# First batch's q and k read as four tokens to a partition and turned by products with the identity

## The chip, the cores and the metric

One core of a Trainium2 chip runs the whole program. The metric is the device time of one execution in microseconds; the time of a kernel is the median of its runs. Times inside an execution come from the hardware profiler, counted from the first instruction.

## The reference

Three stages follow one another on 2304 tokens (4 batches of 576), all in float32:

```python
scores = (q @ k^T) / sqrt(64)                    # q, k, v: 4 batches, 8 heads, 576 tokens, 64 wide
cum    = cumsum(log(clip(f, 1e-4, 1)))           # along the tokens of a head
attn   = softmax(causal(scores + cum[i] - cum[j])) 
x      = (attn @ v) with heads side by side      # 2304 x 512
h      = x @ moe_w_in;  y = (h * tanh(softplus(h))) @ moe_w_out
out    = max(y @ w1, y @ w2, y @ w3) @ moe2_w_out
```

The inputs moe_w_in and the other weights come as 64-bit floats and are converted on the chip.

## The kernel before

The attention runs over 16 jobs, each a pair of heads of one batch; jobs 0 to 3 are the first batch. Here they are called pair 0, pair 1 and so on; pair 4 is the first of the second batch. The steps of a pair:

- `load` (L253) issues the pair's loads on SyncE's queue. For k and then q, two transfers of 128 KB, one for each head (L258), bring the first 512 tokens into the tile raw: 128 partitions hold token p of each of four groups of 128 tokens, so each descriptor moves one token of one head, 64 floats or 256 bytes. The two heads lie side by side in every group. A transfer of 32 KB (L262) brings the last 64 tokens. Then come the decay rows, broadcast to all partitions from cum_d, a scratch tensor that the opening computes from f: c2 (L272, two transfers of 256 KB) and c4 (L275, two of 144 KB), both named cb in the profile. raw and both cb tiles have two buffers, so pair 2 is loaded into what pair 0 has released, and so on.
- `prep` (L301) turns k and q on TensorE: four 128 x 128 transposes into one PSUM bank (L312, tile tr), each of which turns both heads of a group of tokens, and one transpose of the last 64 tokens (L313). ScalarE copies the bank to SBUF (L314, tiles kT and qT: head 0 in partitions 0 to 63, head 1 in 64 to 127, tokens in order along the free dimension). Then v is loaded (L319, L323), and GpSimd masks the decay rows (L295, L299).
- `scores` (L338) multiplies q and k in pieces (L336, tile sc); VectorE adds the decay and finds the row's extreme (L390, it reads cb), ScalarE takes the exponent (L396), VectorE the reciprocals of the sums (L357, L358), GpSimd scales the rows (L360, tile P).
- `av` (L404) transposes P on TensorE (L429, tile pp), copies it to SBUF (L433, L435) and multiplies with v (L415, tile av). The two heads' products write partitions 0 to 63 and 64 to 127 of one bank. A float32 product stands in the trace as two MATMULs, a transpose as one.

Beside the attention `load_w_in` (L198) fetches moe_w_in (L146, tile wr), and converts it: ScalarE takes the high words (L156, which reads every second word), GpSimd and VectorE do the rest (L160 to L170). Two such steps are traced per step of the attention, until all is loaded; the fetches are placed behind the latest split of an attention result on VectorE (`pace`).

Once the 512 tokens of the first block have their attention, products with moe_w_in (L181 to L183) fill TensorE beside the further attention; then follow the two other stages. Before that the opening has no other work for TensorE than the attention of the first batch.

The order of instructions on each engine and queue is not written out by hand: the framework's scheduler orders them by priority along a simulated timeline, when the kernel is built. Each engine and SyncE's queue then work through their list in order, each waiting where it must.

The edit lies in `load` and `prep`; the lines that the steps of the prediction touch are L258 to L275, L312, L314, L156, L146, L336, L390 and L415.

```python
raws = [[ap_.tile([128, 640], F32, name=f"raw{c}{i}") for c in "qk"] for i in range(2)]
c2 = as_.tile([128, 2, 7, 128], F32, name="cb", bufs=2)
c4 = as_.tile([128, S], F32, name="cb4", bufs=2)
```

Of the kernel before, what the change touches and what calls it, by code (L numbers as in the profile page):

```python
# [13 lines left out]
AF = mybir.ActivationFunctionType  # L14
# [50 lines left out]
def tile_decay_attention__mish_ff__max3_ff(  # L65
# [16 lines left out]
    nc = tc.nc  # L82
# [19 lines left out]
    ident = const.tile([128, 128], F32, name="ident")  # L102
# [73 lines left out]
    def queued(last):  # L176
        return tc.issue_after(last[-1].ins) if last else ExitStack()
# [52 lines left out]
    def att_psum(name):  # L230
        return aps.tile([128, 512], F32, name=name, tag="ps", bufs=3)

    U, L = slice(0, 64), slice(64, 128)
# [19 lines left out]
    def load(i, b, hp):  # L253

        raw = raws[i % 2]
        for dst, src in ((raw[1], k), (raw[0], q)):
            for h in range(2):
                nc.sync.dma_start(  # L258
                    dst[:, 0:512].rearrange("p (t h d) -> p t h d", h=2, d=64)[:, :, h],
                    src[b, 2 * hp + h, 0:512, :].rearrange("(t p) d -> p t d", t=4),  # L260
                )
            nc.sync.dma_start(  # L262
                dst[U, 512:640].rearrange("p (h d) -> p h d", h=2),
                src[b, 2 * hp:2 * hp + 2, 512:S, :].rearrange("h p d -> p h d"),
            )
        r = b * H + 2 * hp


        c2 = as_.tile([128, 2, 7, 128], F32, name="cb", bufs=2)
        for t in range(2):  # L270
            src = cum_d[r:r + 2, t * 256:t * 256 + 256][None].to_broadcast([128, 2, 256])
            nc.sync.dma_start(c2[:, :, 3 * t:3 * t + 2, :].rearrange("p h t c -> p h (t c)"), src)  # L272
        c4 = as_.tile([128, S], F32, name="cb4", bufs=2)
        for h, rows in enumerate((U, L)):
            nc.sync.dma_start(c4[rows], cum_d[r + h:r + h + 1, :].to_broadcast([64, S]))  # L275
        return dict(i=i, b=b, hp=hp, cb=(c2, c4), raw=raw)
# [15 lines left out]
    def mask_decay(J):  # L292
        c2, c4 = J["cb"]
        for n, src, dst in ((2, 0, 5), (1, 3, 2), (1, 4, 4)):
            nc.gpsimd.affine_select(  # L295
                out=c2[:, :, dst:dst + n, :], in_=c2[:, :, src:src + n, :], pattern=[[0, 2], [0, n], [-1, 128]],
                compare_op=ALU.is_ge, fill=-1e30, base=0, channel_multiplier=1,
            )
        nc.gpsimd.tensor_tensor(out=c4[:, 512:S], in0=c4[:, 512:S], in1=mask4, op=ALU.add)  # L299

    def prep(J):  # L301

        b, hp, raw = J["b"], J["hp"], J["raw"]
        qq = as_.tile([128, 512], F32, name="qT", bufs=2)
        kk = as_.tile([128, S], F32, name="kT", bufs=2)
        last, v_ = q4[J["i"] % 2], vs[J["i"] % 3]
        rest = att_psum("tr")
        for i, dst in ((1, kk), (0, qq)):
            tr = att_psum("tr")
            with queued(last_av):  # L310
                for c in range(4):
                    nc.tensor.transpose(tr[:, c * 128:c * 128 + 128], raw[i][:, c * 128:c * 128 + 128], ident)  # L312
                last_tr[:] = [nc.tensor.transpose(rest[:, i * 64:i * 64 + 64], raw[i][U, 512:640], ident[U, U])]  # L313
            nc.scalar.activation(dst[:, 0:512], tr, AF.Copy)  # L314
        nc.scalar.activation(kk[:, 512:S], rest[:, 64:128], AF.Copy)
        for h, rows in enumerate((U, L)):
            nc.scalar.activation(last[rows, h * 64:h * 64 + 64], rest[rows, 0:64], AF.Copy)
        for h in range(2):
            nc.sync.dma_start(  # L319
                v_[:, h * 256:(h + 1) * 256].rearrange("p (t d) -> p t d", t=4),  # L320
                v[b, 2 * hp + h, 0:512, :].rearrange("(t p) d -> p t d", t=4),
            )
        nc.sync.dma_start(  # L323
            v_[L, 512:640].rearrange("p (h d) -> p h d", h=2),
            v[b, 2 * hp:2 * hp + 2, 512:S, :].rearrange("h p d -> p h d"),
        )
        J.update(q=qq, q4=last, k=kk, vs=v_)
        mask_decay(J)
# [123 lines left out]
    def attention():  # L452


        jobs = [(b, hp) for b in range(B) for hp in range(H // 2)]
        J = {0: load(0, *jobs[0])}
        yield 0
        prep(J[0])
        J[1] = load(1, *jobs[1])
        tok = 0  # L460
        units = [(ji, g) for ji in range(len(jobs)) for g in range(2)]
        pend = []
        for n in range(len(units) + LEAD):
            if n == 6 + LEAD:
                eps.clear()
                early.close()
                eps_h.append(sa.enter_context(tc.tile_pool(name="hps", bufs=2, space=PSUM, reuse_waits="tile")))
            if n < len(units):
                ji, g = units[n]
                pend.append((J[ji], g, scores(J[ji], g)))  # L470
            if n >= LEAD:
                unit = pend.pop(0)
                rest = av(*unit)
                next(rest)
                if unit[0]["b"] == 0:
                    next(rest, None)
            last_tr.clear()
            if n < len(units) and g == (ji == 0) and ji + 1 < len(jobs):
                prep(J[ji + 1])
            if n >= LEAD:  # L480
                next(rest, None)
                if unit[0]["hp"] == H // 2 - 1:
                    tok = unit[0]["b"] * S + (256, S)[unit[1]]
            if n < len(units):
                if g == 1 and ji + 2 < len(jobs):
                    J[ji + 2] = load(ji + 2, *jobs[ji + 2])
            yield tok
# [340 lines left out]
    for t0 in (BLK2, BLK2 + 2 * HALF):  # L828
        hh = [hp2.tile([128, 2 * HALF], F32R, name=f"hh{c}") for c in range(NF2)]
        hl = [hp2.tile([128, 2 * HALF], F32R, name=f"hl{c}") for c in range(NF2)]  # L830
        for p in range(3):
            fs = slice(p * 128, p * 128 + 128)
            for m in range(3):
                S = []
                for k in range(4):
                    t = sst.tile([128, 2, 2, 128], F32R, name="s")
# [49 lines left out]
            for i, eng in ((0, "pool"), (2, "dve"), (1, "dve"), (3, "dve")) if p == 2 else ((i, "pool") for i in range(4)):  # L886
                f, h = p + 3 * (i // 2), i % 2
# [37 lines left out]
```

## Time and profile before

| what | value |
|---|---|
| median of 3 runs | 909.84 us (909.51 to 910.46) |
| the profiled execution's own time | 909.78 us |
| its span, first to last instruction | 907.7 us |
| mean granted TensorE clock | 0.992 |
| busy: TensorE, VectorE, ScalarE, GpSimd | 97%, 55%, 44%, 26% |

How to read the rows further down. PE is TensorE, PEld its weight load, DVE VectorE, ACT ScalarE, POOL GpSimd, SP SyncE; SPq is SyncE's queue of DMA issues. In a row of a timeline stand the start in us, the time in us (from the first to the end of the last of the instructions merged in it), engine, line, operation, out<-in, the size, and the count; in brackets the idle time before it and what ended it. In the stretches each engine's busy us and number of instructions are followed by PEclk, the clock that TensorE was granted (1.00 is 2.4 GHz, 0.50 is 1.2 GHz), by the mean busy share of the 16 DMA engines, and by GB/s. In the rows by line three numbers of ns are the shortest, the median and the longest.

### The profile page before, as it was taken

The numbers are of one execution on the slowest core, as the hardware profiler recorded it, in microseconds if no ns is written. First come the engines' busy times: TensorE is split into PE (matmuls) and PEld (weight loads), VectorE is DVE, ScalarE is ACT, GpSimd is POOL, SyncE is SP. The second block draws the span as 40 slices with busy tenths as digits, with TensorE's granted clock in tenths as the row PEclk, the third lists the DMA queues.
The fourth block names the chain that finished last, engine by engine and source line by source line (L and its number), as shares of the span: only waits on it lengthen the run. The fifth ranks groups of instructions, "written<-read, shape, count | busy, mean of one in ns | idle before, by whom it ended". The sixth has DMA issues, their size and how long they took to land.

```text
span 907.7 us, 13930 instructions
## 1 busy us (share of the span) xinstructions
PE 882.8 (97%) x4800; PEld 704.8 (78%) x4800; DVE 497.1 (55%) x1186; ACT 400.7 (44%) x913; POOL 232.7 (26%) x317
## 2 busy tenths in 40 slices
PE   6898999999999999999999999999999999999998
PEld 3565666767767778889888888889888998889986
DVE  3598675344444343991367575775855447424440
ACT  4687666454443432533465545553433222412211
POOL 3689987222222220000020000000121332013310
PEclk8989999999999999999999999999999999999999
DMA  7896664444333115863456666663499444333401
GB/s 183 227 226 171 179 192 117 115 134 127 105 102 108 47 48 178 292 226 128 143 181 217 214 216 222 217 226 98 162 359 322 124 123 117 111 96 126 139 23 60
DMA packets 125030, 145.25 MB, mean 160 GB/s; under 512 B 64736, under 2 KB 78048, under 8 KB 124960
## 3 DMA queue, kind: packets, MB, share of 16 engines
q1 hardware_dynamic: 105856, 102.41, 39.0%
q10 hardware_dynamic: 16416, 27.79, 8.3%
q0 software_dynamic: 2688, 14.16, 4.3%
q8 instruction: 38, 0.62, 0.3%
q14 instruction: 32, 0.26, 0.1%
HBM read 102.83 MB, written 41.49 MB: 159 GB/s over the span
## 4 chain that ended last, share of the span: by engine, by line
PE 89%; POOL 3%; DMA 2%; DVE 2%; issue 1%; ACT 1%; SPq 1%; POOLq 0%
PE y L181 7%; PE y L183 7%; PE y L182 7%; PE h L181 7%; PE h L182 7%; PE h L183 7%; PE q L182 6%; PE q L183 6%; PE q L181 6%; PE sc L336 5%; PE av L415 5%; PE pp L429 5%; PE o L181 3%; PE o L182 3%; PE o L183 3%; PE g L181 2%
## 5 line engine op out<-in xcount | busy, mean ns | idle before, releaser
L181 PE MATMUL h<-xh,wi 128*128 128x512 f32 (+1 forms) x320 | 121.4, 380 | 1.6 <-ACT he L522 1.3
L182 PE MATMUL h<-xl,wi 128*128 128x512 f32 (+1 forms) x320 | 120.6, 377 | 1.8 <-DVE xl L137 1.8
L183 PE MATMUL h<-xh,wi 128*128 128x512 f32 (+1 forms) x320 | 120.7, 377 | 0.0
L182 PE MATMUL y<-gl,wo 128*128 128x512 f32 (+1 forms) x320 | 117.7, 368 | 0.0
L183 PE MATMUL y<-gh,wo 128*128 128x512 f32 (+1 forms) x320 | 117.6, 368 | 0.0
L181 PE MATMUL y<-gh,wo 128*128 128x512 f32 (+1 forms) x320 | 106.3, 368 | 0.0
L360 POOL TENSOR_SCALAR P<-P,rr 128x128 f32<-128x128 f32 (+3 forms) x128 | 74.0, 592 | 87.5 <-DVE rr L358 31.5
L659 DVE TENSOR_TENSOR gl<-g,gh 128x512 fp32r<-128x512 f32 x72 | 50.0, 697 | 83.3 <-ACT gh L658 83.1
L396 ACT ACTIVATE P<-P,mn 128x128 f32<-128x128 f32 (+3 forms) x128 | 70.7, 554 | 53.4 <-DVE mn L390 50.2
L652 ACT ACTIVATE g<-g 128x512 f32<-128x512 f32 x72 | 45.2, 632 | 70.6 <-DMA g<-h_d 65.7
L181 PEld LDWEIGHTS h<-xh,wi 128*128 128x128 f32 x320 | 60.1, 188 | 14.6 <-issue 2.2
L182 PEld LDWEIGHTS h<-xl,wi 128*128 128x128 f32 x320 | 60.1, 188 | 14.0 <-issue 2.8
L183 PEld LDWEIGHTS h<-xh,wi 128*128 128x128 f32 x320 | 60.3, 188 | 11.5 <-issue 2.7
L182 PEld LDWEIGHTS y<-gl,wo 128*128 128x128 f32 x320 | 60.3, 188 | 10.2
L183 PEld LDWEIGHTS y<-gh,wo 128*128 128x128 f32 x320 | 60.2, 188 | 10.1
L181 PEld LDWEIGHTS y<-gh,wo 128*128 128x128 f32 x320 | 60.3, 189 | 10.1
L522 ACT ACTIVATE he<-h 128x512 f32<-128x512 f32 x56 | 33.3, 595 | 57.0 <-PE h L183 52.4
L851 DVE TENSOR_TENSOR u<-q,p 128x448 f32<-128x448 f32 x36 | 22.4, 621 | 62.3 <-PE q L183 60.7
L336 PE MATMUL sc<-kT,qT 64*128 64x128 f32 (+3 forms) x256 | 51.9, 500 | 3.6 <-DVE mn L390 3.3
L429 PE MATMUL pp<-ident,P 128*128 128x128 f32 x320 | 51.1, 285 | 4.0 <-ACT qT L314 3.6
L658 ACT ACTIVATE gh<-g 128x512 fp32r<-128x512 f32 x72 | 45.0, 627 | 22.0 <-PE y L183 20.9
L429 PEld LDWEIGHTS pp<-ident,P 128*128 128x128 f32 x320 | 37.0, 143 | 20.1 <-issue 5.0
(141 smaller groups left out, 1850.3 us busy)
## 6 DMA issues: line engine op xcount, KB each, us to landing
g<-h_d SPq DMA_DIRECT2D x72, 256.0 KB, 2.9
s<-s_d SPq DMA_DIRECT2D x72, 256.0 KB, 3.0
h_d<-he ACTq DMA_DIRECT2D x56, 256.0 KB, 2.9
wr<-in_moe_w_out_dram SPq DMA_DIRECT2D x22, 512.0 KB, 4.6
wr<-in_moe_w_dram SPq DMA_DIRECT2D x24, 384.0 KB, 3.8
s_d<-sk POOLq DMA_DIRECT2D x12, 768.0 KB, 5.8
cb<-cum_d SPq DMA_DIRECT2D x32, 256.0 KB, 4.2
wr<-in_moe_w_in_dram SPq DMA_DIRECT2D x16, 512.0 KB, 4.5
```

The costliest lines, as they stand in the source:

```text
L181: nc.tensor.matmul(ps, wh, xh, start=start, stop=False, skip_group_check=True)
L182: nc.tensor.matmul(ps, wh, xl, start=False, stop=False, skip_group_check=True)
L183: return nc.tensor.matmul(ps, wl, xh, start=False, stop=stop, skip_group_check=True)
L336: nc.tensor.matmul(dst, lhs, J["k"][rows, c0:c0 + w], start=True, stop=True, skip_group_check=True)
L360: nc.gpsimd.tensor_scalar(made[ci], made[ci], rr[:, ci:ci + 1], 1.0, op0=ALU.mult, op1=ALU.mult)
L396: nc.scalar.activation(Pt, Pt, AF.Exp, scale=-1.0, bias=mn[:, col - 1:col], accum_out=sm[:, ci:ci + 1],)
L415: last = nc.tensor.matmul(acc[(U, L)[h], off:off + w], J["vs"][:, n * 64:n * 64 + 64], T[:, at[h]:at[h] + w], start=kt == 0 and off == 0, ...
L429: turn = nc.tensor.transpose(pp[:, n * 128:n * 128 + 128], Pt[:, k0:k0 + 128], ident)
L522: nc.scalar.activation(he, h, AF.Copy)
L652: nc.scalar.activation(g, g, AF.Mish)
L658: on_act[:] = [nc.scalar.activation(gh, g, AF.Copy)]
L659: on_dve[:] = [nc.vector.tensor_tensor(out=gl, in0=g, in1=gh, op=ALU.subtract)]
```

## The change

For jobs of the first batch (b is 0) the transfers of q and k's first 512 tokens place four consecutive tokens in one partition, 256 floats or 1 KB in a row, head by head in the two halves of the tile. The transpose of 128 columns then no longer holds both heads of one group; instead each of the four tokens of each head is turned by a float32 product with the identity (64 columns of weights, 128 moving columns), which writes the half of the bank that belongs to the head. In the bank the columns then stand as token-in-four first; the copy out of PSUM reads them in order and writes them with a step of four words, so that kT and qT hold what they held before. The last 64 tokens, the later batches and all else stay.

```diff
         for dst, src in ((raw[1], k), (raw[0], q)):
             for h in range(2):
+                if b == 0:
+                    nc.sync.dma_start(
+                        dst[:, h * 256:h * 256 + 256],
+                        src[b, 2 * hp + h, 0:512, :].rearrange("(p t) d -> p (t d)", t=4),
+                    )
+                    continue
                 nc.sync.dma_start(
                     dst[:, 0:512].rearrange("p (t h d) -> p t h d", h=2, d=64)[:, :, h],
                     src[b, 2 * hp + h, 0:512, :].rearrange("(t p) d -> p t d", t=4),
...
                 for c in range(4):
-                    nc.tensor.transpose(tr[:, c * 128:c * 128 + 128], raw[i][:, c * 128:c * 128 + 128], ident)
+                    cs = slice(c * 128, c * 128 + 128)
+                    if b:
+                        nc.tensor.transpose(tr[:, cs], raw[i][:, cs], ident)
+                        continue
+                    for h, rows in enumerate((U, L)):
+                        part = raw[i][:, h * 256 + c * 64:h * 256 + c * 64 + 64]
+                        nc.tensor.matmul(tr[rows, cs], part, ident, start=True, stop=True, skip_group_check=True)
...
-            nc.scalar.activation(dst[:, 0:512], tr, AF.Copy)
+            if b:
+                nc.scalar.activation(dst[:, 0:512], tr, AF.Copy)
+            else:
+                nc.scalar.activation(
+                    dst[:, 0:512].rearrange("r (p c) -> r c p", c=4), tr.rearrange("r (c p) -> r c p", c=4), AF.Copy
+                )
```

## Rows read from the trace of the kernel before

**Rows 1.** Busy us of TensorE, its share of the span, instructions.
```profile
PE 882.8 (97%) x4800; PEld 704.8 (78%) x4800; DVE 497.1 (55%) x1186; ACT 400.7 (44%) x913; POOL 232.7 (26%) x317
```

**Rows 2.** Stretches of the opening: busy us by engine, clock, DMA.
```profile
10.00:20.00 10.00, 6.75 (x24) 3.77 (x22) 3.28 (x19) 4.78 (x17) 3.17 (x7) 0.72 0.98 233
41.77:45.38 3.61, 0.00 (x1) 0.00 (x1) 1.04 (x5) 2.45 (x7) 2.33 (x3) 0.97 1.03 367
45.20:51.50 6.30, 6.12 (x27) 4.37 (x27) 6.12 (x21) 5.65 (x19) 4.14 (x4) 0.50 1.05 238
```

**Rows 3.** The chain of waits from 37 to 44 us: start, us, what.
```profile
37.07 0.59 SPq L146
...
37.70 6.46 DMA wr<-in_moe_w_in_dram
```

**Rows 4.** Timelines of ScalarE and TensorE around 42 to 46 us.
```profile
42.48 0.66 ACT L156 ACTIVATE wt<-wr 128x512 f32<-128x512 f32 x1 [3.85 <-DMA wr<-in_moe_w_in_dram]
...
45.38 1.11 PE L429 MATMUL pp<-ident,P 128*128 128x128 f32 x4 [3.61 <-ACT qT L314]
```

**Rows 5.** Timeline of SyncE's queue, from pair 1's second k to pair 3's q.
```profile
10.01 0.59 SPq L258 DMA_DIRECT2D rawk<-in_k_dram  x1
...
20.87 0.61 SPq L262 DMA_DIRECT2D rawq<-in_q_dram  x1
21.57 1.19 SPq L275 DMA_DIRECT2D cb<-cum_d  x2
...
23.50 0.96 SPq L272 DMA_DIRECT2D cb<-cum_d  x2
...
25.75 1.74 SPq L258 DMA_DIRECT2D rawk<-in_k_dram  x2
...
28.48 1.75 SPq L258 DMA_DIRECT2D rawq<-in_q_dram  x2
```

**Rows 6.** Issues by line: L258 to 38 us, L649 in all, L649 in one run.
```profile
L258 SPq DMA_DIRECT2D rawk<-in_k_dram x10: 410/541/1156, 1.2 to 31.6; - x10
L258 SPq DMA_DIRECT2D rawq<-in_q_dram x10: 497/524/1203, 3.0 to 33.5; - x10
...
L649 SPq DMA_DIRECT2D g<-h_d x64: 314/320/790, 355.3 to 585.6; - x64
...
L649 SPq DMA_DIRECT2D g<-h_d x5: 424/492/790, 355.3 to 357.7; - x5
```

**Rows 7.** Stretches of one us: q and k's rows; then the decay's.
```profile
3.00:4.00 1.00, 0.00 (x0) 0.00 (x0) 0.25 (x2) 0.68 (x1) 0.00 (x0) 1.00 0.70 159
...
10.00:11.00 1.00, 1.00 (x8) 0.36 (x4) 0.00 (x0) 0.00 (x0) 0.00 (x0) 1.00 0.95 310
```

**Rows 8.** Timeline of TensorE: turns of pairs 1 and 2, products av.
```profile
14.33 1.02 PE L312 MATMUL tr<-ident,rawk 128*128 128x128 f32 x4 [3.25 <-issue]
...
15.58 1.12 PE L312 MATMUL tr<-ident,rawq 128*128 128x128 f32 x4
...
23.05 0.60 PE L312 MATMUL tr<-ident,rawk 128*128 128x128 f32 x4
...
30.88 1.08 PE L415 MATMUL av<-TB,vs 128*64 128x256 f32 x8
```

**Rows 9.** Timeline of VectorE: it reads pair 0's scores and decay.
```profile
11.99 0.29 DVE L390 CUSTOM_DVE_ANT_0 P<-sc,cb 128x128 f32<-128x128 f32 x1 [6.06 <-POOL cb L295]
...
19.87 0.52 DVE L390 CUSTOM_DVE_ANT_0 P_None<-sc,cb,mn 128x288 f32<-128x288 f32 x1 [0.15 <-DVE mn L390]
...
21.89 0.69 DVE L390 CUSTOM_DVE_ANT_1 P<-sc,cb 128x512 f32<-128x512 f32 x1
```

**Rows 10.** ScalarE's groups by shape: a plain copy, a read of every second word.
```profile
L435 ACT ACTIVATE TB<-pp 128x512 f32<-128x512 f32 x32 | 18.7, 587 | 8.5 <-PE pp L429 8.5
...
L156 ACT ACTIVATE wt<-wr 128x512 f32<-128x512 f32 x16 | 10.7, 671 | 9.2 <-POOL wi L137 4.8 <-DMA wr<-in_moe_w_in_dram 4.3
```

## The prediction

> **What bounds the kernel now.** I read the busy table first: TensorE is busy for 882.8 of 907.7 us [rows 1], so after the opening nothing is won except by giving TensorE its work earlier. The change touches the first batch alone, so the next view is the opening itself, in stretches: from 41.77 to 45.38 us TensorE did nothing, and from 45.2 to 51.5 it worked at a granted clock of 0.50, the lower level (1.2 GHz) [rows 2]. The chain of waits and the engines' timelines say why. The first w_in rows are issued at 37.07 and land 6.46 us later; ScalarE stands in its queue at their conversion (idle 3.85 us), and the copy qT of pair 3 (the fourth head pair), which TensorE waits for, is queued behind it [rows 3, 4]. So the event that starts the rest is the w_in issue, and it comes when SyncE has worked through its list: from 10.01 us on SyncE issues one DMA after another, all loads of pairs 1 to 4 [rows 5]. An earlier w_in issue, and no later arrival of TensorE at 41.77, is what a gain would be made of.
>
> **The sum's base.** The profiled execution took 909.78 us, 2.08 more than its span of 907.70, and 0.06 less than the median of the three runs.
>
> **Part 1, the issues of q and k on SyncE.** One issue of the old form took 0.52 to 0.54 us at the median, with two stretched to 1.16 and 1.20; the kernel has 128-row issues of one plain run per partition (g) at 0.32 at the median, and 0.42 to 0.79 where five follow each other at once [rows 6]. The new form is such a plain one. Bounds for it: 0.32 and 0.53. I take 0.42, the lowest of the dense group, since these too follow at once: 0.11 saved each. Seven of them (three of pair 1, four of pair 2) stand between 10.01 and 21.57, where SyncE issues pair 2's decay rows: 0.77 us. Pair 3's four take 1.74 + 1.75 = 3.49 us [rows 5]; at 0.42 with 0.05 between two they take 1.78, a saving of 1.71; if the two stretched ones stay stretched, 2 x 0.11, say 0.25. I take 1.0, the middle.
>
> **Part 2, the transfer.** In a stretch with 256-byte rows of q and k the queues moved 159 GB/s at a share of 0.70, so 227 at full share; with the decay's 1-KB rows 310 at 0.95, so 326 [rows 7]. The four long transfers of a pair, 524 kB, fall from 2.31 to 1.61 us of all engines: 0.70 per pair. Bounds: 0 and 0.70. Pair 1's two k transfers give half of it: TensorE starts pair 1's turn 0.35 us earlier. Pair 0's are hidden: VectorE stood 6.06 us waiting for the decay before it read pair 0's first scores [rows 9]. In front of w_in the queue holds pair 4's rows, which stay at 256 bytes, so I take nothing there and keep 0.70 for the low end.
>
> **Part 3, the turn on TensorE.** Four transposes become eight fp32 products, each of which runs as two MATMULs of 128 columns: 16 x 128 columns, in pairs for the two halves of the output. The nearest row is av, eight MATMULs of 256 columns, as many columns in the same two halves: 1.08 us at the higher clock level, against 0.60 for four transposes [rows 8]. So 0.48 more per turn. If the halves do not overlap, twice the columns' time: about 1.9, so 1.3 more. Below 0.48 I see nothing. Pair 1's turns ran at the lower level, 1.02 and 1.12 us [rows 8], about 1.8 times the 0.60: 0.87 more each, 1.74 for both, less the 0.35 of part 2: 1.39. Behind them on TensorE stand the last scores of pair 0, whose readers on VectorE end at 20.39 and 22.58 [rows 9] and free the two decay buffers that pair 2 is loaded into. These ends move to 21.78 and 23.97. SyncE, ready 0.77 earlier, must therefore wait: pair 2's two decay loads go from 21.57 to 21.78 and from 23.50 to 23.97 [rows 5]. **The early saving is eaten, and 0.47 is added.** Pairs 2 and 3 add 0.96 each on TensorE before 41.77.
>
> **Part 4, the copies.** The copy out of PSUM is 0.59 us and now writes one word in four. No row shows such a write. The nearest is w_in's conversion, which reads every second word: 671 against 587 ns for a plain copy of the same size [rows 10]. I take +0.08, hidden for pairs 0 to 2 (ScalarE was 4.78 us busy of 10 to 20 us, [rows 2]), 0.08 on the path for pair 3's qT. Bounds: 0 and +0.59, a doubling.
>
> **The sum.** At the w_in issue: +0.47 - 1.0 = -0.53, so TensorE is released at 45.38 - 0.53 + 0.08 = 44.93. TensorE itself arrives at 41.77 + 0.47 + 2 x 0.96 = 44.16. The idle of 3.61 us shrinks to 0.8, filled by the turn's own extra products. The granted clock fell behind the two idle stretches of over 3 us in the opening, this one and the 3.25 us before 14.33 [rows 2, 8]; with 0.8 us I expect it to stay at 1.00, the higher level (2.4 GHz). Of the 6.3 us that follow at 0.50 [rows 2] half, 3.1, would come back if TensorE alone set the pace; VectorE is 6.12 of 6.30 us busy there, so I take a third, 1.0 (bounds 0 and 3.1). Sum: -0.45 - 1.0, about -1.5 on the span: 906.2, with 2.08 around it 908.3 us. What follows is moved along, since TensorE is the bound there.
>
> **Rival A, the stretched issues were the queue's own backlog.** Short rows fill the queue, SyncE waits for room; with a quarter of the rows both stretched issues go: -1.71 instead of -1.0. If pair 1's eight products also run faster than at the lower level, its buffers come free about 0.8 earlier than I reckoned, w_in meets 0.7 us less data, and the clock gives 1.5: -1.71 - 0.3 - 0.7 - 1.5 = -4.2, 905.6 us. For it: issues beside full queues are the long ones [rows 5, 6]. Against: pair 2's issue of the 32-KB rest of q, with a quarter of the rows, took 0.61, no less than a long one [rows 5].
>
> **Rival B, slower: TensorE arrives after its release.** TensorE has 44.93 - 41.77 = 3.16 us to spend before the release point. If the two halves don't overlap, pairs 2 and 3 alone add 4 x 1.3 = 5.2, and pair 1 delays the decay loads by up to 4: TensorE arrives at about 47 or later, +1.6 with nothing passed on from pair 1, +5 with all of it. I take +2.5, 912.3 us. It decides where the extra products before 41.77 pass 3.16 us, 0.8 per turn. Against it: av's halves do overlap in the row [rows 8].
>
> **Rival C, the strided copy.** If a copy takes 1.17 us instead of 0.59, six copies of pairs 1 to 3 add 3.5 us to ScalarE; pair 2's two are in the path of its scores, pair 3's qT delays TensorE by 0.59: about 1.8 in all, which turns -1.5 into +0.3, 910.1 us. The Trainium skill, "SBUF — State Buffer", section "Door 1: The DMA port swizzle", says that SBUF is reached in lines of 16 bytes and that full bandwidth wants at least two hits in a line; here every word written goes to a line of its own. By that rule this rival holds; no row here shows such a write.
>
> **Rival D, it does not do what it says.** Issues cost the same, the queue drains as before, the products hide in the idle stretch: 0, 909.8 us.
>
> **How the numbers follow.** A measurement of this kernel tells about 0.2%, 1.8 us, so faster is below 908.0. The forecast has 0.40; its own range, 906.2 to 909.8, lies on both sides of that bound: 0.16 faster, 0.24 within. A has 0.24, all faster. B has 0.20, all slower. C has 0.09, 0.07 within and 0.02 slower. D has 0.07, within. Together: faster 0.40, within 0.38, slower 0.22. The range for 8 times in 10 takes in A's centre and most of B: 905.0 to 912.2.
>
> **What would show it.** Right: q and k issues near 0.42 us; the first w_in issue near 36.5; a turn of about 1.1 us for pair 2; TensorE's idle before pair 3's qT under 1.5 us and the clock at 1.00 from 45 to 51 us. Wrong: turns of 1.9 us (B), copies above 0.8 us (C), unchanged issues (D). It is also wrong if the list on SyncE or ScalarE comes out in another order, above all if qT no longer stands behind the w_in conversion.

## The result and the profile after the change

The changed kernel takes 915.75 us at the median of 4 runs (915.06 to 916.95), beside 910.15 for the kernel before on the same chip (909.51 to 910.56): ratio 1.0064, 95% interval [1.0046, 1.0081]. It is slower by 5.6 us, where 1.5 us faster was forecast; 915.75 also lies outside the range, 905.0 to 912.2. The profiled execution took 915.83 us, its span is 914.1, against 907.7 before.

**Span = busy TensorE + idle TensorE** is the first reading. The page's busy row, which answers to [rows 1]:

```profile
PE 890.1 (97%) x4896; PEld 711.4 (78%) x4896; DVE 497.0 (54%) x1186; ACT 402.2 (44%) x913; POOL 234.7 (26%) x317
```

TensorE is 890.1 us busy where it was 882.8: +7.3. Its idle time is 914.1 - 890.1 = 24.0 where it was 24.9: -0.9. The two make the 6.4 us of the span. So no new wait is the loss in sum; TensorE has more to do, and the waits that were to cover it did not shrink by as much. Next, where. The view by stretches (busy us of TensorE, its weight load, VectorE, ScalarE, GpSimd; granted clock; DMA share; GB/s), the kernel before and then the changed one:

```profile
0.00:160.00 160.00, 139.94 (x903) 93.38 (x904) 108.87 (x342) 102.97 (x290) 121.83 (x161) 0.96 0.70 185
160.00:425.00 265.00, 265.00 (x1645) 201.79 (x1644) 130.23 (x384) 114.75 (x297) 47.64 (x92) 1.00 0.42 132
```

```profile
10.00:20.00 10.00, 7.22 (x54) 4.24 (x50) 5.09 (x25) 6.49 (x20) 3.19 (x7) 1.00 0.98 235
20.00:30.00 10.00, 7.40 (x38) 4.40 (x38) 1.14 (x6) 2.74 (x6) 4.74 (x11) 0.66 0.67 194
30.00:40.00 10.00, 10.00 (x77) 6.13 (x73) 8.20 (x39) 8.97 (x27) 5.69 (x11) 1.00 0.81 237
40.00:50.00 10.00, 7.30 (x74) 4.58 (x72) 8.75 (x27) 6.95 (x21) 9.73 (x13) 0.99 0.75 221
50.00:60.00 10.00, 9.40 (x46) 5.63 (x47) 6.88 (x29) 8.95 (x27) 9.92 (x14) 0.67 0.89 199
0.00:160.00 160.00, 140.66 (x966) 94.41 (x967) 106.66 (x334) 102.66 (x281) 121.89 (x157) 0.96 0.66 179
160.00:425.00 265.00, 265.00 (x1629) 200.87 (x1628) 130.81 (x390) 114.52 (x302) 49.60 (x96) 1.00 0.42 134
```

From 160 to 425 us both kernels keep TensorE full at a clock of 1.00, and behind 425 us it idles 4.6 us, 4.8 before. So the difference arises in the first 160 us, and over these TensorE idles about as long as before (19.3 us against 20.1), at the same mean clock of 0.96. What it did in that busy time is the difference. Two thirds of the loss stand by the first product of h, which starts at 65.6 us (61.5 before); the last one starts at 430.7 us (424.2). The timeline of TensorE shows the turns of the first three pairs (of pair 2 only k) and the new waits (start, us, line, operation, count, idle before and its releaser; these answer to [rows 8]):

```profile
3.59 2.21 PE L324 MATMUL tr<-ident,rawk 128*64 128x128 f32 x16 [3.59 <-DMA rawk<-in_k_dram]
...
6.03 1.98 PE L324 MATMUL tr<-ident,rawq 128*64 128x128 f32 x16
...
13.70 1.45 PE L324 MATMUL tr<-ident,rawk 128*64 128x128 f32 x16 [1.57 <-DMA rawk<-in_k_dram]
...
15.28 1.09 PE L324 MATMUL tr<-ident,rawq 128*64 128x128 f32 x16
...
21.00 0.33 PE L446 MATMUL pp<-ident,P 128*128 128x128 f32 x1 [2.20 <-POOL P L377]
22.93 0.90 PE L446 MATMUL pp<-ident,P 128*128 128x128 f32 x3 [1.60 <-POOL P L377]
23.76 1.97 PE L324 MATMUL tr<-ident,rawk 128*64 128x128 f32 x14
...
27.86 0.69 PE L324 MATMUL tr<-ident,rawk 128*64 128x128 f32 x2
...
50.11 1.09 PE L446 MATMUL pp<-ident,P 128*128 128x128 f32 x4 [2.81 <-POOL P L377]
51.69 1.65 PE L353 MATMUL sc<-kT,qT 64*128 64x128 f32 x8 [0.49 <-ACT qT L329]
```

A turn is 1.09 us at the higher clock level and about 2 us at the lower: 14 of the 16 MATMULs of pair 2's k take 1.97 us at a granted clock of 0.50.

```profile
23.76:25.73 1.97, 1.97 (x16) 1.64 (x16) 0.00 (x0) 0.00 (x0) 0.00 (x0) 0.50 0.47 139
```

Pair 0's two turns last about as long as at that level; the trace has no record of the clock so early. Adding up all rows of the eight turns in this timeline gives 15.0 us, in the kernel before 7.1: +7.9, all of the added busy time (7.3) and a little more. The idle of 3.61 us ahead of 45.38 is gone, but other stretches stand in its place: 2.20 and 1.60 us at 21 and 23 us, 2.81 at 50 us, all for GpSimd's scaling of P. The first two come of TensorE being early: at the higher level it is done with its scores at 18.80 us, while GpSimd starts that scaling at 20.57 us, no earlier than before (20.32). The clock fell there in turn (0.66 in 20 to 30, 0.67 in 50 to 60).

SyncE's queue (answering to [rows 3, 5]):

```profile
20.69 0.61 SPq L268 DMA_DIRECT2D rawq<-in_q_dram  x1
21.35 1.14 SPq L336 DMA_DIRECT2D vs<-in_v_dram  x2
22.53 0.61 SPq L340 DMA_DIRECT2D vs<-in_v_dram  x1
23.24 1.19 SPq L281 DMA_DIRECT2D cb<-cum_d  x2
24.52 0.53 SPq L259 DMA_DIRECT2D rawk<-in_k_dram  x1
25.15 1.98 SPq L278 DMA_DIRECT2D cb<-cum_d  x2
27.23 0.42 SPq L259 DMA_DIRECT2D rawk<-in_k_dram  x1
...
28.46 1.02 SPq L259 DMA_DIRECT2D rawq<-in_q_dram  x2
...
34.31 2.44 SPq L146 DMA_DIRECT2D wr<-in_moe_w_in_dram  x4
```

Two things are to be seen. The list has another order: pair 2's v now goes ahead of its decay rows, which are issued at 23.24 and 25.15 instead of 21.57 and 23.50. And w_in, which was to start everything, is issued at 34.31, earlier by 2.76 us, without a gain. ScalarE's groups by shape (answering to [rows 10]) show the copies:

```profile
L452 ACT ACTIVATE TB<-pp 128x512 f32<-128x512 f32 x32 | 18.8, 593 | 24.2 <-PE pp L446 24.2
...
L327 ACT ACTIVATE qT<-tr 128x512 f32<-128x512 f32 x12 | 7.2, 598 | 11.7 <-PE tr L320 11.4
...
L329 ACT ACTIVATE kT<-tr 128x512 f32<-128x512 f32 x4 | 4.4, 1096 | 3.9 <-PE tr L324 3.9
L329 ACT ACTIVATE qT<-tr 128x512 f32<-128x512 f32 x4 | 4.4, 1091 | 1.1 <-PE tr L324 1.1
```

A strided copy takes 1.09 us, a plain one 0.59 to 0.60.

### The profile page after: what moved, and what is told of

The parts are those of the page before. It is cut to its first block, busy times and chain, and to the rows that moved or that the text cites. A ratio compares the mean times of both kernels' runs of the same rounds, so it can differ in the third digit from the quotient of the medians.

```text
span 914.1 us, 14136 instructions
## 1 busy us (share of the span) xinstructions
PE 890.1 (97%) x4896; PEld 711.4 (78%) x4896; DVE 497.0 (54%) x1186; ACT 402.2 (44%) x913; POOL 234.7 (26%) x317
## 4 chain that ended last, share of the span: by engine, by line
PE 88%; POOL 4%; ACT 2%; DVE 2%; issue 2%; DMA 1%; SPq 0%; POOLq 0%; DVEq 0%; ACTq 0%
PE y L181 7%; PE y L183 7%; PE y L182 7%; PE h L181 7%; PE h L182 7%; PE h L183 7%; PE q L182 6%; PE q L181 6%; PE q L183 6%; PE sc L353 5%; PE pp L446 4%; PE av L432 4%; PE o L181 3%; PE o L182 3%; PE o L183 3%; PE g L181 2%
## 5 line engine op out<-in xcount | busy, mean ns | idle before, releaser
L377 POOL TENSOR_SCALAR P<-P,rr 128x128 f32<-128x128 f32 (+3 forms) x128 | 76.1, 608 | 98.2 <-DVE rr L375 54.3
L182 PEld LDWEIGHTS y<-gl,wo 128*128 128x128 f32 x320 | 60.3, 189 | 10.2
L432 PE MATMUL av<-TB,vs 128*64 128x64 f32 (+2 forms) x576 | 48.8, 288 | 1.4 <-DVE xl L137 1.4
```

The lines of the kernel that those rows point to most:

```text
L182: nc.tensor.matmul(ps, wh, xl, start=False, stop=False, skip_group_check=True)
L377: nc.gpsimd.tensor_scalar(made[ci], made[ci], rr[:, ci:ci + 1], 1.0, op0=ALU.mult, op1=ALU.mult)
L432: last = nc.tensor.matmul(acc[(U, L)[h], off:off + w], J["vs"][:, n * 64:n * 64 + 64], T[:, at[h]:at[h] + w], start=kt == 0 and off == 0, ...
```

## The experiments

Three theories: **copy** (C; the strided copy holds up what stands behind it), **lists** (O; the scheduler writes other lists for all engines, and these are worse; called order or relisting below), **products** (P; TensorE's added time counts). In tables, busy and idle are TensorE's in the profiled execution, idle being span less busy; the ratio is to the kernel before, run beside it. Span, busy and idle of the kernel before are those of its profile above.

### The parts one at a time

The copy alone, on the kernel before. The tokens within a pair's qT and kT then come in another order, so scores and P belong to other tokens. All engines' lists are those of the kernel before.

```diff
-            nc.scalar.activation(dst[:, 0:512], tr, AF.Copy)
+            if b:
+                nc.scalar.activation(dst[:, 0:512], tr, AF.Copy)
+            else:
+                nc.scalar.activation(
+                    dst[:, 0:512].rearrange("r (p c) -> r c p", c=4), tr.rearrange("r (c p) -> r c p", c=4), AF.Copy
+                )
```

> The kernel before with nothing changed but the copy: for the first batch it writes with a step of four words (so the tokens of kT and qT stand in another order than the reference's). Every engine's and queue's list is that of the kernel before, instruction by instruction. Theory C (the copy makes the loss): each of the eight copies takes about 1.09 us instead of 0.60, 4 us more on ScalarE, most of it on the path: 913 to 914 us. Theory O (the lists that the scheduler made for the changed kernel make the loss): the copies of pairs 0, 1 and 3 hide in front of waits, only pair 2's two are on the path: 910.3 to 911.3 us.

The changed kernel with the plain copy again (that diff's first line in place of the rest; the token order differs here too). Its lists are those of the changed kernel.

> The changed kernel with a plain copy: the copy writes in order (tokens of the first batch's kT and qT stand in another order). Every list is that of the changed kernel. Theory C: the loss goes, 911 to 912 us. Theory O: the lists stay, so the loss stays but for the copies that are on the path (kT and qT of pair 3, one after the other in front of the scores at 51.7 us): 914 to 915 us.

The 1-KB loads alone, with the old transposes and the plain copy (the turned blocks then hold other tokens and heads):

```diff
             for h in range(2):
+                if b == 0:
+                    nc.sync.dma_start(
+                        dst[:, h * 256:h * 256 + 256],
+                        src[b, 2 * hp + h, 0:512, :].rearrange("(p t) d -> p (t d)", t=4),
+                    )
+                    continue
```

> The loads alone: 1-KB rows, but the old four transposes and the plain copy (kT and qT then hold two tokens of one head where one token of two heads should stand). The scheduler makes a list of its own, in which pair 2's decay loads stand ahead of its v. My forecast's terms: 9 to 11 issues at 0.42 to 0.50 instead of 0.53, 0.5 to 1.5 us earlier at the w_in issue: 908.5 to 910 us. Theory O in its strong form (any new list may lose some us): 910 to 914, and the trace then shows a wait that the kernel before has not. Theory P (the extra products make the loss) and C: below 910.

The products alone, on rows loaded as before, with the plain copy; this computes the reference:

```diff
-                    nc.tensor.transpose(tr[:, c * 128:c * 128 + 128], raw[i][:, c * 128:c * 128 + 128], ident)
+                    cs = slice(c * 128, c * 128 + 128)
+                    if b:
+                        nc.tensor.transpose(tr[:, cs], raw[i][:, cs], ident)
+                        continue
+                    for h, rows in enumerate((U, L)):
+                        part = raw[i][:, c * 128 + h * 64:c * 128 + h * 64 + 64]
+                        nc.tensor.matmul(tr[rows, cs], part, ident, start=True, stop=True, skip_group_check=True)
```

> The products alone: 256-byte rows as before, the turn by eight float32 products with the identity for the first batch, plain copy; what is computed is the reference's. The scheduler makes a list of its own, with pair 2's decay loads ahead of its v. Theory P (16 x 128 columns instead of 4 x 128 per turn, 0.48 us each at the higher clock level, 0.87 at the lower): 912 to 914 us. Theory O: the products fill TensorE's idle times: 909.5 to 911.5 us. If real products bring the clock up earlier, pair 1's turn shows 1.1 to 1.5 us for k and TensorE runs at 2.4 GHz before 21 us.

| kernel | median us | ratio, 95% interval | span | busy | idle |
|---|---|---|---|---|---|
| before | 909.82 | | 907.7 | 882.8 | 24.9 |
| copy alone | 910.31 | 1.0006 [0.9997, 1.0015] | 907.8 | 883.9 | 23.9 |
| changed, plain copy | 916.41 | 1.0073 [1.0060, 1.0086] | 913.0 | 888.8 | 24.2 |
| loads alone | 914.01 | 1.0049 [1.0036, 1.0061] | 911.9 | 884.7 | 27.2 |
| products alone | 911.21 | 1.0018 [1.0009, 1.0027] | 910.6 | 890.1 | 20.5 |

**Copy falls.** A dearer copy costs nothing that can be told from zero, and taking it out gives nothing back (916.41 us, where the theory had 911 to 912). Loads alone cost 4 us although none of their instructions got dearer: that speaks for lists. Products alone have the full +7.3 us of busy time, and 4.4 us less idle covers part of it: 911.21 us lies in the range expected of lists, below the 912 to 914 of products. Pair 1's k, which was to show an earlier rise of the clock by 1.1 to 1.5 us, took 0.66 + 1.97 us there, as at the lower level; in the changed kernel it took 1.45.

### One swap in the list, with all else held

Pair 2's decay rows are issued behind pair 2's v, as in the changed kernel; the other lists stay as before, but for GpSimd's, where that pair's mask steps move behind steps that scale P.

```diff
-        return dict(i=i, b=b, hp=hp, cb=(c2, c4), raw=raw)
+        return dict(i=i, b=b, hp=hp, raw=raw, cb=None if (b, hp) == (0, 2) else load_cb(b, hp))
...
+        if J["cb"] is None:
+            with tc.issue_after(v_last.ins):
+                J["cb"] = load_cb(b, hp)
```

> The kernel before, in which one thing is changed: pair 2's decay rows are issued on SyncE behind pair 2's v instead of ahead of it, as in the changed kernel. Every other list stays as before. In the changed kernel's trace TensorE stood idle 2.20 us at 21.0 us and 1.60 us at 22.9 us for GpSimd's scaling of P, which had waited 4.98 us for those rows (2.65 before). Theory order (this one swap is the loss of the opening): about 2 to 4 us slower than before, 912 to 914 us, with these two idle stretches in it. Theory relisting (the loss is spread over the whole new lists and this swap is a small part): within 1 us of before, 909.5 to 911 us.

910.95 us, 1.0009 [1.0000, 1.0018]: 1.0 us, at most 1.6 by the end of the interval. The two idle stretches at 21 to 23 us measure 0.33 and 0.75 us here, not 2.20 and 1.60:

```profile
20.92 0.33 PE L435 MATMUL pp<-ident,P 128*128 128x128 f32 x1 [0.33 <-POOL P L366]
22.84 0.55 PE L435 MATMUL pp<-ident,P 128*128 128x128 f32 x3 [0.75 <-POOL P L366]
```

But these two stretches are no sign of the swap: GpSimd starts the scaling that TensorE waits for there at 20.50 us, and at 20.57 in the changed kernel. What the late rows hold up is a later scaling. In the changed kernel and in the kernel before it stands behind a mask of those rows in GpSimd's list, in this run ahead of it:

```profile
28.30 0.31 POOL L305 TENSOR_TENSOR cb<-cb,mask 128x64 f32<-128x64 f32 x1 [4.98 <-DMA cb<-cum_d]
28.59 1.37 POOL L377 TENSOR_SCALAR P<-P,rr 128x512 f32<-128x512 f32 x2
```

```profile
25.71 0.30 POOL L299 TENSOR_TENSOR cb<-cb,mask 128x64 f32<-128x64 f32 x1 [2.65 <-DMA cb<-cum_d]
26.00 1.36 POOL L360 TENSOR_SCALAR P<-P,rr 128x512 f32<-128x512 f32 x2
```

```profile
24.92 1.36 POOL L366 TENSOR_SCALAR P<-P,rr 128x512 f32<-128x512 f32 x2 [1.67 <-ACT TA L441]
```

So the swap costs about 1 us, at most 1.6, where GpSimd's list goes round it; what it costs in the changed kernel this run does not settle. TensorE there does not idle between 23.76 and 47 us, so no wait directly behind the late scaling shows.

### The same work under other lists

One line decides which of q and k of a pair is loaded first. It adds no instruction, but with it the scheduler writes all lists anew:

```diff
-        for dst, src in ((raw[1], k), (raw[0], q)):
+        for dst, src in ((raw[1], k), (raw[0], q))[::-1 if b == 0 and hp >= 2 else 1]:
```

This went into the kernel before, the loads alone and the changed kernel, in the second list below. In the third list it is `hp >= 1` for the first two, and all pairs of the first batch for the changed kernel.

> The kernel before with the same work in another order of lists: for pairs 2 and 3 the loads of q are issued ahead of those of k. Nothing else is changed, no instruction is added or gets dearer, but the scheduler then writes the lists of all engines anew (about as many lines move as between before and after). Theory relisting (which list the scheduler happens to write is worth microseconds by itself): the time moves away from before by over 0.2%, to either side, by 2 to 6 us. Theory work (the loss is in the work that the change does: loads that land earlier, products, the strided copy): within 0.2% of before, 908 to 911.7 us.

> The 1-KB loads alone (old transposes and plain copy, the contents differ), with the same swap as in the other run: q of pairs 2 and 3 loaded ahead of k. Theory relisting: the 4.2 us that the loads alone had cost belong to one list, and with another list they need not come back; the time moves by over 2 us from 914.0, most likely towards before, 908 to 912 us. Theory work (1-KB loads cost by themselves, for instance because a stage of h that starts earlier meets a full GpSimd): it stays at 913 to 915 us.

> The changed kernel with the same swap: q of pairs 2 and 3 loaded ahead of k. Theory relisting: moves by over 2 us from 915.75, to either side; 908 to 920 us. Theory work: 914.5 to 917 us, and by the runs so far the products alone would hold 1.4 us of it over before, the copy 0.5 us.

> The kernel before with q loaded ahead of k for pairs 1 to 3 (the run before this one did it for pairs 2 and 3): same work, a third set of lists. Theory relisting: anywhere in 905 to 918 us, and not within 1 us of both earlier sets (910.0 and 916.75). If instead the swap itself costs the 6.8 us (q ahead of k is late for TensorE, which turns k first), this kernel, which swaps one pair more, takes 916 us or more.

> The 1-KB loads alone (old transposes, plain copy, contents differ), q ahead of k for pairs 1 to 3: a third set of lists. Theory relisting: in 904 to 916 us, set by TensorE's idle time and low-clock time in the first 160 us (22.8 us in both sets so far by one sum, 26.6 in the kernel before). If the 1-KB loads gain by themselves once the list doesn't stand against it: under 909 us as in the last run of them.

> The changed kernel with q loaded ahead of k for all four pairs of the first batch: a third set of lists for it. Theory relisting with the products' price beside it (8 us of TensorE time in every kernel that has them): lists may give back some of it, 910 to 920 us; it should stay over 908 us, since even the best list so far with cheap turns took 906.6. If the products cost next to nothing by themselves, a list as good as the best one would bring it under 908 us.

The products alone, under a second list (pairs 2 and 3 swapped) and a third (all four):

> The products with identity alone (old loads, plain copy; what is computed is that of the reference), with q of pairs 2 and 3 loaded ahead of k: another set of lists. Theory products (they add about 8 us to TensorE's time and most of it shows, with the lists moving each kernel by some us to either side): 913 to 921 us, turns at 30 to 31 us of TensorE time. Theory lists only (the products hide, as the 911.2 us of the first set suggest): 905 to 913 us.

> The products with identity alone, with q of all four pairs of the first batch loaded ahead of k: a third set of lists. Theory products: 913 to 921 us; both this one and the run before it under 912 would speak against it. Theory lists only: 905 to 913 us.

| work | list | median us | ratio, 95% interval | span | busy | idle |
|---|---|---|---|---|---|---|
| before | 2 | 916.75 | 1.0073 [1.0061, 1.0086] | 914.5 | 886.0 | 28.5 |
| before | 3 | 910.68 | 1.0020 [1.0008, 1.0033] | 908.7 | 883.0 | 25.7 |
| loads | 2 | 906.61 | 0.9964 [0.9951, 0.9976] | 904.2 | 883.3 | 20.9 |
| loads | 3 | 915.25 | 1.0058 [1.0045, 1.0071] | 914.4 | 885.8 | 28.6 |
| products | 2 | 916.94 | 1.0076 [1.0062, 1.0090] | 914.7 | 886.4 | 28.3 |
| products | 3 | 918.97 | 1.0097 [1.0083, 1.0111] | 917.6 | 887.2 | 30.4 |
| changed | 2 | 918.70 | 1.0095 [1.0080, 1.0111] | 915.5 | 887.9 | 27.6 |
| changed | 3 | 924.98 | 1.0169 [1.0155, 1.0183] | 923.1 | 892.9 | 30.2 |

**The lists are shown to be a cause by themselves, as large as the change.** The kernel before, with the same instructions in another order, is 6.8 us slower: more than the change itself. The swap as such is not it, since the third list swaps one pair more and is 6 us faster than the second. The loads, 4.2 us slower under their first list, are 3.4 faster than the kernel before under their second, and 5.8 slower again (915.25 against 909.41 beside it) under the third. On the mean of three lists each, the loads alone take 912.0 us and the kernel before 912.4: by themselves they show neither a price nor a gain. Three of these runs went further than I had expected of any list (the kernel before and the loads under list 2, the changed kernel under list 3), and the third list of the kernel before came out nearer to its first than I had expected. A row of the second list of the kernel before, by stretches, shows what a worse list looks like:

```profile
45.00:59.00 14.00, 12.84 (x44) 6.64 (x45) 8.71 (x30) 10.17 (x29) 10.83 (x15) 0.51 0.87 202
```

TensorE is at the lower level for 14 us, where [rows 2] has 6.3 us of it, after an idle stretch of 4.09 us at 44.93:

```profile
44.93 1.62 PE L429 MATMUL pp<-ident,P 128*128 128x128 f32 x8 [4.09 <-ACT kT L314]
47.71 1.65 PE L336 MATMUL sc<-kT,qT 64*128 64x128 f32 x8 [1.16 <-ACT qT L314]
```

The list of the fast one (loads, list 2) has three short waits in that place:

```profile
41.53 0.63 PE L435 MATMUL pp<-ident,P 128*128 128x128 f32 x4 [0.80 <-ACT kT L320]
42.73 0.66 PE L435 MATMUL pp<-ident,P 128*128 128x128 f32 x4 [0.57 <-ACT q L323]
44.24 1.65 PE L342 MATMUL sc<-kT,qT 64*128 64x128 f32 x8 [0.86 <-ACT qT L320]
```

A long stretch at the lower level alone does not make a list bad, though, for this fast one has 10 us of it:

```profile
43.50:53.80 10.30, 9.56 (x27) 4.58 (x27) 8.13 (x27) 6.51 (x21) 8.34 (x11) 0.50 0.97 217
```

**Products are the other cause, as far as six against six can show.** Without them (before and loads, three lists each) busy time is 882.8 to 886.0 us; with them (products and changed, three each) 886.4 to 892.9. The two sets don't overlap, and their means differ by 889.1 - 884.3 = 4.8 us. All work on the tile tr, the turns of the whole program, takes 27.4 to 28.4 us without and 34.7 to 37.0 with, whatever the list: +7.4 on the mean, so the rest of TensorE's work took 2.6 less. Idle time does not make it good: its means are 26.0 without and 26.8 with. The medians average 912.2 and 917.8; there the sets overlap (906.6 to 916.8, 911.2 to 925.0), so their difference of 5.6 us is an estimate from these means, not a price.

### Parts of the change in parts of the kernel

The stride moved from the copy to the products (`tr[rows, c:512:4]` in place of `tr[rows, cs]`, and the plain copy), with the lists of the changed kernel:

> The changed kernel with the stride moved from the copy to the products: each product writes its columns of the PSUM bank with a step of four floats, and ScalarE copies the bank plainly. The lists of all engines stay those of the changed kernel. Theory relisting (the loss against before is in the lists and in TensorE's 8 us for the products): 915 to 917 us, as with the changed kernel, the copy at 0.60 us and a turn at 1.09. If a strided write of PSUM is dear as the strided write of the copy was, a turn takes 2 us or more instead of 1.09 and the time rises to 918 us or more.

914.36 us, 1.0056 [1.0042, 1.0069]: not to be told from the changed kernel, if a little under the 915 expected. Its products last as long as before (272 to 473 ns each, against 272 to 476 in the changed kernel), and its copies 0.59 us: writing PSUM with a step cost nothing that shows, writing SBUF with a step nearly doubled the copy.

The whole change for pair 0 alone (`b == 0 and hp < 1` in place of `b == 0`, and the old form elsewhere), then for pairs 0 and 1 (`hp < 2`):

> The whole change for pair 0 alone (its q and k in 1-KB rows, products, strided copy); pairs 1 to 3 as in the kernel before. The lists of the engines stay nearly those of before (four lines of TensorE's list differ). Pair 0's turns take 2.2 and 2.0 us instead of 1.1 each, but behind them VectorE waits for the decay anyway. Theory price-by-place (a product's TensorE time counts only where no wait covers it): 909 to 911 us, within 0.2% of before. Theory strict (every TensorE microsecond counts): 911.5 to 912.5 us.

> The whole change for pairs 0 and 1, pairs 2 and 3 as in the kernel before; the lists are new. TensorE's time for turns should rise by about half of the 8 us of the whole change, or less. Relisting alone moved kernels of the same work between 3.4 us faster and 6.8 slower. Expected 907 to 917 us, and by the sum of TensorE's time by kind: turns near 26 to 27 us (22.8 before, 30.9 after), the rest idle and low-clock time.

Pair 0 alone: 911.40 us, 1.0017 [1.0007, 1.0027], 1.3 us slower; between the two theories' ranges, so neither holds as stated. Its turns take 2.34 and 1.85 us, yet the first product of h starts at 61.5 us in both kernels, so up to there the time was covered. Busy time is 2.3 us more in the profile, about what pair 0's turns added (tile tr: 30.5 us against 28.1). Far behind, from 109 to 115 us, the clock was 0.72 here and 1.00 before; but it was 0.74 in the copy alone too, whose span is that of the kernel before, so this is not shown to be a price of the change:

```profile
109.00:115.00 6.00, 6.00 (x26) 4.91 (x25) 4.07 (x12) 3.96 (x11) 5.92 (x7) 0.72 0.57 152
```

Pairs 0 and 1: 915.94 us, 1.0058 [1.0044, 1.0073], under lists of its own; busy 887.9, idle 26.8. The turns take 31.7 us (tile tr), about half of the whole change's addition, as expected, and yet it is no better than the whole change. No kernel here that computes the reference beat the kernel before.

## Why the prediction was wrong

**The failing step is in the sum: "The idle of 3.61 us shrinks to 0.8, filled by the turn's own extra products".** The products' time was found, and then costed at nothing because a wait would cover it. What the runs showed in its place: the turns took 7.9 us more, that wait went away, and others came, so that TensorE idles 24.0 us instead of 24.9. The cover did not outlast the new order of the work. The sum should have carried the added busy time in full, with the change of idle time as its unknown. From the rows at hand, turns at 1.08 for 0.60 give eight times 0.48, 3.8 us; with half of them at the lower level, at the 0.87 that Part 3 used, 5.4.

**The second failing step is "What follows is moved along", and before it, that every list keeps its order.** I named another order as what would make the forecast wrong, but gave it no price and no chance. The price is now measured: between its three lists the span of the same work differs by 6.8 us (kernel before), 10.2 (loads), 7.0 (products) and 9.0 (changed kernel). Nor does the opening carry on one to one: with the loads alone under their first list the first h starts at 57.5 us, 4.0 earlier than before, and the last one at 426.0, 2.0 later.

The parts, in order.

- **Part 1** was near in the piece and without use in the whole. An issue takes 0.43 us (k) and 0.47 (q) at the median; 0.42 was taken. Pair 3's four take 0.53 + 0.42 + 1.02 = 1.97 us, against 1.78 forecast and 3.49 before: the stretched issues went, as Rival A had it. The w_in issue came at 34.31, where 36.5 was forecast; how much of that is the new order is not shown. That w_in is "the event that starts the rest" fell: TensorE next waits for GpSimd.
- **Part 2**: pair 1's k is turned at 13.70 instead of 14.33, 0.63 earlier, where 0.35 was taken.
- **Part 3** had the size at the higher level right, 1.09 for 1.08. Its chain of delay failed. Pair 1's turns, priced at the lower level with 1.74 us more for both, ran at the higher and took 1.45 and 1.09 us, 0.40 more. VectorE's last reads of pair 0's scores and decay end at 18.91 and 20.15 us, earlier than before, where 21.78 and 23.97 was forecast:

```profile
18.39 0.52 DVE L407 CUSTOM_DVE_ANT_0 P_None<-sc,cb,mn 128x288 f32<-128x288 f32 x1
...
19.46 0.69 DVE L407 CUSTOM_DVE_ANT_1 P<-sc,cb 128x512 f32<-128x512 f32 x1
```

  Pair 2's decay rows are late all the same, by 1.67 and 1.65 us instead of 0.21 and 0.47: v stands in front of them in the list.
- **Part 4** was mis-sized: +0.08 taken, +0.49 measured; the bound of +0.59 held. It costs nothing to be seen, since the changed kernel is as slow with the plain copy. The forecast of a clock that stays up failed too: it was 0.99 from 40 to 50 us, but 0.67 from 50 to 60, and over the first 160 us 0.96 as before, so the 1.0 us that the sum took for it did not come.
- **Rival B** has the right sign by another way: the halves do overlap, at 1.09 us, and TensorE is not late for one release; it simply has more to do. **Rival C** has the dearer copy and not the loss: the copies take 1.07 to 1.13 us, but neither adding nor removing their step moves the time. The Trainium skill, "SBUF — State Buffer", section "Door 1: The DMA port swizzle", says that each access that goes on to a new line of 16 bytes pays a penalty; the copies' time agrees. **Rival A**'s shorter issues came, and pair 1's products did run at the higher level; its gain did not come. **Rival D** fell: the change does what it says.

**What stays open:** why one list is good and another bad. Idle time, its places and the low-clock stretches differ all through the first 160 us, and no single wait that I tried accounts for it. How the 5.6 us of this change divide between products and list can't be settled either: busy time says products (+7.3), and other lists move the same work as far. What the late decay rows cost by way of GpSimd's list is open too.

## What to carry to other kernels

Where TensorE is 97% busy, read a change first as span = busy + idle: count what it adds to busy time in full, at the clock level of the place, and let a wait cover it only if that wait would outlast a new order of the work. Where a scheduler writes the lists, a change of loads or products can draw a new one for every engine (here a dearer copy alone did not); before a few microseconds are put down to a change, measure this spread, by running the same work under two or three other lists. A wait that ends last in one list is no lasting bound of the kernel.

## What was not expected of the hardware

- **A copy to SBUF with a step.** ScalarE's 128x512 fp32 copy out of PSUM takes 1.09 us when it writes one word in four, and 0.60 when it writes in a row. With the step in TensorE's writes to PSUM neither the products nor the copy slow down.
- **The granted clock falls at different places under the same lists.** From 20 to 30 us it was 0.66 in the changed kernel and 1.00 with the stride in PSUM, of the same lists; the 14 MATMULs of pair 2's k that took 1.97 us in the one took 1.09 in the other. From 109 to 115 us it was 1.00 in the kernel before and 0.74 in the copy alone, whose spans are 907.7 and 907.8. I had read the falls as coming behind idle stretches of over 3 us; in the changed kernel it fell behind stretches of 2.20 and 1.60. The row with the stride in PSUM:

```profile
23.55 1.09 PE L324 MATMUL tr<-ident,rawk 128*64 128x128 f32 x14
```

- **A stretch at the lower level can cost nothing.** The kernel before comes to its first product with P at 21.16 us without a wait, after 4 us and more at a clock of 0.50; the changed kernel, at 1.00 there, is early, waits 2.20 us for GpSimd, and starts the same product at 21.00:

```profile
21.16 0.35 PE L429 MATMUL pp<-ident,P 128*128 128x128 f32 x1
```

- **A clock of 1.00 in a row can stand for no record.** The first record of the clock lies at 11.0 us in the trace of the kernel before and at 20.0 us in that of the copy alone, and rows count the time ahead of it as 1.00. So the copy alone shows 1.00 from 14 to 22 us, where the kernel before shows 0.57; yet pair 1's turns take 1.09 and 1.11 us in it, as long as the 1.02 and 1.12 at the lower level in [rows 8]. Here the time of a known instruction tells the level, not the row:

```profile
14.00:22.00 8.00, 7.43 (x23) 3.91 (x23) 4.21 (x22) 6.29 (x18) 3.91 (x10) 1.00 1.08 215
```

```profile
14.45 1.09 PE L312 MATMUL tr<-ident,rawk 128*128 128x128 f32 x4 [2.79 <-issue]
...
15.76 1.11 PE L312 MATMUL tr<-ident,rawq 128*128 128x128 f32 x4
```
